# A lambda table made in parts between Vector products, one k copy moved to Scalar and one mask product postponed, in a linear-attention and gated-FFN kernel

## The chip, the cores and the metric

One core of one Trainium2 chip. The metric is the device time of one execution in microseconds (us). The profile names the engines PE (TensorE), DVE (Vector), ACT (Scalar), POOL (GpSimd) and SP. "Span" is the time from the first to the last instruction that the trace shows.

## The reference, cut to what matters

Block-wise linear attention with a decay lambda per head (4 batches, 8 heads, 768 positions, width 64), then a gated feed-forward layer on the result.

```python
Dmask = np.where(rel >= 0, lam[:, None, None] ** rel[None, :, :], 0.0)
lam_pow = lam[:, None, None] ** (pos[None, :, None] + 1)
for b in range(nb):
    intra = np.einsum('bhic,bhjc->bhij', qb, kb) * Dmask[None]
    intra = np.einsum('bhij,bhjd->bhid', intra, vb)
    inter = np.einsum('bhid,bhde->bhie', qb * lam_pow[None], kv_state)
    out[:, :, sl] = intra + inter
    # ... kv_state is decayed and updated
gate = 1.0 / (1.0 + np.exp(-(x @ w_gate)))
val = x @ w_val
return (gate * val @ w_out)
```

## The kernel before

It works on six blocks of 128 positions. q is scaled by a table of powers of lambda, `lamq`. Block 0 has a table of its own; the table for later blocks is made on Vector while the first block's units ("unit tile" = 128 columns of the hidden layer: matmuls g and v, sigmoid, product) run.

```python
def make_lamq():
    lp = const.tile([128, HP, C], FP32, tag="lp")
    for u in range(2):                       # two column copies
        us = slice(u * 64, (u + 1) * 64)
        nc.vector.tensor_copy(lp[us]...[:, :, :, 0], lam_bc[us, :]...[:, u])
    w = 1
    while w < C:                             # seven doublings
        nc.vector.tensor_tensor(out=lp[:, :, w:2 * w], in0=lp[:, :, 0:w],
                                in1=lp[:, :, w - 1:w].to_broadcast([128, HP, w]), op=ALU.mult)
        w *= 2
    nc.vector.tensor_copy(lamq, lp)          # the cast to bf16
# ... the order of block 0
piece_tq0([1]); piece_tk0(0)     # transposes; piece_tk0 copies k to SBUF: i=0 of pair 0 on Vector, else Scalar
make_mask(1); idle(1)
piece_s(0, [0]); piece_m(0, 0)   # scores of batch 0, times the mask (two Vector products)
piece_s(0, [1]); piece_m(0, 1)
piece_tk0(1)
piece_tq0([2]); piece_tq0([3])   # transposes of q and their scaling on Vector
piece_s(0, [2], ps_ff, "ff"); piece_m(0, 2)
piece_s(0, [3]); piece_m(0, 3)
# ... later: GpSimd issues the loads of weights and of block 1, each when an earlier one has landed
load_gv(3, GW); load_gv(4, GW); load(1, "qk", 0, 2); load_gv(5, GW)  # ...
# ... units of block 0
make_lamq()
for ft in (2, 3): gs[ft] = psum(); mm_part(gs[ft], WG, ...); sigm(0, ft, gs[ft])
for ft in (2, 3): vp = psum(); mm_part(vp, WV, ...); prod(0, ft, vp)
g4 = psum(); mm_part(g4, WG, ...); sigm(0, 4, g4)
v4 = psum(); mm_part(v4, WV, ...); prod(0, 4, v4)
```

`psum()` takes a buffer from a pool of three. v4 can start only when the product of tile 2 has been made.

Of the kernel before, what the change touches and what calls it, by code (L numbers as in the profile page):

```python
# [7 lines left out]
FP32 = mybir.dt.float32  # L8
BF16 = mybir.dt.bfloat16
# [6 lines left out]
def kernel(  # L16
# [11 lines left out]
    nc = tc.nc  # L28

    B, H, S, D = q.shape  # L30
    C = 128
    NSTEP = S // C
    HP = H // 2
# [7 lines left out]
    const = ctx.enter_context(tc.tile_pool(name="const", bufs=1))  # L41
# [3 lines left out]
    mtp = ctx.enter_context(tc.tile_pool(name="mtp", bufs=4))  # L45
# [57 lines left out]
    def load_wo(i, w):  # L103
        fs = slice(i * w, (i + 1) * w)
        nc.gpsimd.dma_start(out=WO[:, fs, :], in_=wo_r[:, fs, :])
# [14 lines left out]
    w = 1  # L120
# [38 lines left out]
    for u in range(2):  # L159
        us = slice(u * 64, (u + 1) * 64)  # L160
# [10 lines left out]
    for u in range(2):  # L171
        us = slice(u * 64, (u + 1) * 64)
# [3 lines left out]
    lamq = const.tile([128, HP, C], BF16, tag="lamq")  # L176
    mask = const.tile([128, H, C], FP32, tag="mask")

    def make_lamq():
        lp = const.tile([128, HP, C], FP32, tag="lp")  # L180
        for u in range(2):
            us = slice(u * 64, (u + 1) * 64)
            nc.vector.tensor_copy(lp[us].rearrange("p (e x) c -> p e x c", e=2)[:, :, :, 0],
                                  lam_bc[us, :].rearrange("p (x u e) -> p u e x", u=2, e=2)[:, u])
        w = 1
        while w < C:
            nc.vector.tensor_tensor(out=lp[:, :, w:2 * w], in0=lp[:, :, 0:w],  # L187
                                    in1=lp[:, :, w - 1:w].to_broadcast([128, HP, w]), op=ALU.mult)
            w *= 2
        nc.vector.tensor_copy(lamq, lp)  # L190

    def make_mask(u):
# [4 lines left out]
    def masked(out, x, n, u):  # L197
        if n == 0:
            nc.vector.tensor_tensor(out=out, in0=x, in1=mask[:, u::2, :], op=ALU.mult)  # L199
            return  # L200
        nc.vector.tensor_tensor(  # L201
            out=out.rearrange("p (e x) c -> p e x c", e=2), in0=x.rearrange("p (e x) c -> p e x c", e=2),
            in1=mask.rearrange("p (x u e) c -> p u e x c", u=2, e=2)[:, u], op=ALU.mult)
# [7 lines left out]
    QS, KS, MT, XT, KD = {}, {}, {}, {}, {}  # L211
# [22 lines left out]
    def transpose_pair(out, x, b, g):  # L234
        nc.tensor.transpose(out, x[:, b, 2 * g:2 * g + 2, :].rearrange("p h d -> p (h d)"), ident)
# [7 lines left out]
    def piece_tq0(bs, then=None):  # L243
        tq = ps_at.tile([128, 2, 2, 2 * C], BF16, name="tq", tag="ps")
        for b in bs:
            if (0, b // 2) not in QS:
                QS[0, b // 2] = trsb.tile([128, 2, 2, 2, C], BF16, tag="QS", name="QS")
            for g in range(HP):
                transpose_pair(tq[:, b % 2, g // 2, g % 2 * C:g % 2 * C + C], Q[0], b, g)
        if then:  # L250
            then()
        for b in bs:
            nc.vector.tensor_tensor(out=QS[0, b // 2][:, :, b % 2].rearrange("p e x c -> p e (x c)"),
                                    in0=tq[:, b % 2], in1=lamq0_e, op=ALU.mult)

    def piece_tk0(bp):
        tk = ps_at.tile([128, 2, 2, 2 * C], BF16, name="tk", tag="ps")
        for i in range(2):
            for g in range(HP):
                transpose_pair(tk[:, i, g // 2, g % 2 * C:g % 2 * C + C], K[0], 2 * bp + i, g)  # L260
        KS[0, bp] = trsb.tile([128, 2, 2, 2, C], BF16, tag="KS", name="KS")
        for i in range(2):
            cp = nc.vector.tensor_copy if bp == 0 and i == 0 else nc.scalar.copy
            cp(KS[0, bp][:, :, i].rearrange("p e x c -> p e (x c)"), tk[:, i])

    def piece_t(n, bp):
        if n > 1 or bp == 1:
# [21 lines left out]
    def piece_s(n, bs, pool=ps_at, tag="ps"):  # L289

        for b in bs:
            bp, i = b // 2, b % 2
            sp = [pool.tile([128, HP, C], FP32, name=f"sp{u}", tag=tag) for u in range(2)]
            for hp in range(HP):
                for u in range(2):
                    us = slice(u * 64, (u + 1) * 64)
                    nc.tensor.matmul(sp[u][:, hp, :], lhsT=KS[n, bp][us, hp // 2, i, hp % 2, :],  # L297
                                     rhs=QS[n, bp][us, hp // 2, i, hp % 2, :],
                                     start=(hp == 0), stop=(hp == HP - 1), skip_group_check=True)
            SP[n, b] = sp  # L300

    def piece_m(n, b):
        MT[n, b] = mtp.tile([128, 2, HP, C], BF16, tag="MT", name="MT")
        for u in range(2):
            masked(MT[n, b][:, u], SP[n, b][u], n, u)

    def intra(n, b, out, m, start, stop):
# [68 lines left out]
    def fade():  # L376
        for bp in range(NB2):
            SD[bp] = kdp.tile([128, 2, HP, D], FP32, tag="sd", name="sd", bufs=2)
            nc.gpsimd.tensor_tensor(out=SD[bp], in0=Sb[:, 2 * bp:2 * bp + 2],  # L379
                                    in1=dec.unsqueeze(1).unsqueeze(3).to_broadcast([128, 2, HP, D]),  # L380
                                    op=ALU.mult)
# [6 lines left out]
    def c(n, *pairs):  # L388
        for bp in pairs:
            pool, tag = (ps_at, "ps") if bp == 0 or n == 0 else (ps_ff, "ff")  # L390
            cp = pool.tile([128, 2, HP, D], FP32, name="cp", tag=tag)
            for i in range(2):
                for hp in range(HP):
                    for u in range(2):
                        h = head(hp, u)
                        nc.tensor.matmul(cp[half(u), i, hp, :], lhsT=kdh(n, 2 * bp + i, h),  # L396
                                         rhs=V[n][:, 2 * bp + i, h, :], start=(i == 0 and hp == 0),
                                         stop=(i == 1 and hp == HP - 1), skip_group_check=True)
            dst = Sb[:, 2 * bp:2 * bp + 2]
            if n == 0:  # L400
                nc.vector.tensor_copy(dst, cp)
            else:
                nc.vector.tensor_tensor(out=dst, in0=cp, in1=SD.pop(bp), op=ALU.add)  # L403
# [3 lines left out]
    def piece_gv(n, ft):  # L407
        fs = slice(ft * 128, (ft + 1) * 128)
        x = XT[n].rearrange("p m b c -> p m (b c)")
        gp = ps_ff.tile([128, TCH], FP32, name="gp", tag="ff")  # L410
        for mt in range(NMT):
            nc.tensor.matmul(gp, lhsT=WG[:, mt, fs], rhs=x[:, mt, :],  # L412
                             start=(mt == 0), stop=(mt == NMT - 1))
        sg = htp.tile([128, TCH], BF16, tag="sg", name="sg", bufs=3)
        nc.scalar.activation(sg, gp, AF.Sigmoid)  # L415
        vp = ps_ff.tile([128, TCH], FP32, name="vp", tag="ff")
        for mt in range(NMT):
            nc.tensor.matmul(vp, lhsT=WV[:, mt, fs], rhs=x[:, mt, :],  # L418
                             start=(mt == 0), stop=(mt == NMT - 1))
        HT[n, ft] = htp.tile([128, TCH], BF16, tag="ht", name="ht", bufs=2 * NFT)  # L420
        nc.vector.tensor_mul(HT[n, ft], sg, vp)  # L421

    def mm_part(ps, W, n, ft, lo, hi):
        x = XT[n].rearrange("p m b c -> p m (b c)")
        for mt in range(NMT):
            nc.tensor.matmul(ps[:, lo:hi], lhsT=W[:, mt, ft * 128:(ft + 1) * 128], rhs=x[:, mt, lo:hi],  # L426
                             start=(mt == 0), stop=(mt == NMT - 1))

    def psum():
        return ps_ff.tile([128, TCH], FP32, name="gp", tag="ff")  # L430
# [5 lines left out]
    def prod(n, ft, vp):  # L436
        sg = HT[n, ft]
        HT[n, ft] = htp.tile([128, TCH], BF16, tag="ht", name="ht", bufs=2 * NFT)
        nc.vector.tensor_mul(HT[n, ft], sg, vp)  # L439
# [53 lines left out]
    idle(1)  # L493
    piece_tq0([1])
    piece_tk0(0)
    make_mask(1)
    idle(1)
    piece_s(0, [0])
    piece_m(0, 0)
    piece_s(0, [1])  # L500
    piece_m(0, 1)
    piece_tk0(1)
    nc.scalar.preload_act_table_set("sigmoid_and_others")
    piece_tq0([2])
    piece_tq0([3])
    piece_s(0, [2], ps_ff, "ff")
    piece_m(0, 2)
    piece_s(0, [3])
    piece_m(0, 3)
# [37 lines left out]
    def gv(n, *fts):  # L547
        for ft in fts:
            piece_gv(n, ft)
# [10 lines left out]
    mm_part(v1, WV, 0, 1, 0, TCH)  # L560
    prod(0, 1, v1)
    c(0, 1)
    make_lamq()
    gs = {}
    for ft in (2, 3):
        gs[ft] = psum()
# [2 lines left out]
    for ft in (2, 3):  # L569
        vp = psum()  # L570
        mm_part(vp, WV, 0, ft, 0, TCH)
        prod(0, ft, vp)
    g4 = psum()
    mm_part(g4, WG, 0, 4, 0, TCH)
    sigm(0, 4, g4)
    v4 = psum()
    mm_part(v4, WV, 0, 4, 0, TCH)
    prod(0, 4, v4)
    fade()
    make_kd(1)  # L580
    for i in range(3):
        load_wo(i, NFT // 3)
    gv(0, 5, 6, 7)
    gv(0, 8)
    t(1, 0)
    gv(0, 9)
# [104 lines left out]
```

## Time and profile before

Median 226.81 us of three runs (226.63 to 226.98).

| reading | value | where it is read |
|---|---|---|
| PE busy | 216.0 us of a span of 225.3 (96%) | the page, part 1 |
| PE's share of the chain that ended last | 91% | the page, part 4 |
| largest wait of PE behind 14.7 us | 0.61 us idle, at v of unit tile 4 | the timeline |

From the page of the kernel before, part 1 (busy time, share of the span, instructions) and part 4 (the chain by engine):

```profile
PE 216.0 (96%) x1726; PEld 114.3 (51%) x1748; DVE 106.8 (47%) x193; ACT 79.2 (35%) x149; POOL 78.5 (35%) x77
PE 91%; DVE 3%; DMA 3%; issue 2%; ACT 1%; DVEq 0%; POOLq 0%
```

The timeline of the same run around the table. Columns: start, duration (us), engine, source line, operation, output<-inputs, count, and in brackets the idle time before it and what ended it.

```profile
19.13 0.88 POOL L85 DMA_DIRECT2D qb<-in_q_dram  x1 [0.64 <-DMA WG<-in_moe_w_gate_dram]
20.23 0.87 POOL L85 DMA_DIRECT2D qb<-in_q_dram  x1 [0.23 <-DMA WV<-in_moe_w_val_dram]
20.58 0.68 DVE L183 COPY lp<-lam_bc 64x4 f32<-64x4 f32 x2
21.29 1.84 DVE L187 TENSOR_TENSOR lp<-lp 128x4 f32<-128x4 f32 x7
22.93 0.87 POOL L85 DMA_DIRECT2D kb<-in_k_dram  x1 [0.48 <-DMA WV<-in_moe_w_val_dram]
23.17 0.85 DVE L190 CAST lamq<-lp 128x512 bf16<-128x512 f32 x1
23.95 1.26 DVE L439 TENSOR_TENSOR ht<-sg,gp 128x512 bf16<-128x512 bf16 x2
24.67 1.02 PE L426 MATMUL gp<-XT,WV 128*128 128x512 bf16 x4 [0.61 <-DVE ht L439]
```

Read from the bottom: v4 waited for the product of tile 2, which waited behind the cast. A later section returns to the POOL lines and to the first column copy, which taken alone lasted 0.50 us while its twin of the same shape took 0.17:

```profile
20.58 0.50 DVE L183 COPY lp<-lam_bc 64x4 f32<-64x4 f32 x1
```

The timeline of block 0 in the same run (`tk` transposed k in PSUM, `KS` its copy, `sp` scores, `MT` masked scores, `QS` scaled q), up to the first unit matmul:

```profile
7.39 0.62 PE L235 MATMUL tk<-ident,kb 128*128 128x128 bf16 x8 [0.27 <-DMA kb<-in_k_dram]
8.04 0.42 DVE L264 COPY KS<-tk 128x512 bf16<-128x512 bf16 x1 [0.38 <-PE tk L235]
8.50 0.59 ACT L264 COPY KS<-tk 128x512 bf16<-128x512 bf16 x1 [1.33 <-DVE KS L264]
8.98 2.48 DVE L199 TENSOR_TENSOR MT<-sp,mask 128x512 bf16<-128x512 f32 x4
11.38 0.75 DVE L253 TENSOR_TENSOR QS<-tq,lamq 128x512 bf16<-128x512 bf16 x2
11.85 0.73 PE L297 MATMUL sp<-QS,KS 64*128 64x128 bf16 x16 [0.69 <-DVE QS L253]
12.26 2.48 DVE L199 TENSOR_TENSOR MT<-sp,mask 128x512 bf16<-128x512 f32 x4
14.70 0.49 PE L426 MATMUL gp<-XT,WG 128*128 128x384 bf16 x2
```

Vector is almost never free here; between 11.38 + 0.75 and 12.26 it waited 0.13 us for scores.

### The profile page before, as it was taken

To read this page: it belongs to the slowest core of one execution; us is meant where nothing else is said; L and a number is where in the kernel's file an instruction comes from. 1 tells how busy PE (TensorE), PEld (TensorE's weight loads), DVE (VectorE), ACT (ScalarE), POOL (GpSimd) and SP (SyncE) were. 2 spreads that over 40 slices of the span, in tenths; PEclk is the share of its full clock that TensorE was granted. 3 is DMA by queue.
4 is the path that set the end of the run, shared out by engine and by line. 5 is a ranking of instruction groups with operands and counts; after the bars stand their busy time and mean duration, and the time that the engine had idled before them with its cause. 6 is when DMAs were issued, how large, how long until landed. Compare 5 with 4: busy or idle time off the path is not lost.

```text
span 225.3 us, 4243 instructions
## 1 busy us (share of the span) xinstructions
PE 216.0 (96%) x1726; PEld 114.3 (51%) x1748; DVE 106.8 (47%) x193; ACT 79.2 (35%) x149; POOL 78.5 (35%) x77
## 2 busy tenths in 40 slices
PE   6689899999999999999999999999999999999994
PEld 2454355888854455444545444446444445444443
DVE  7898646586430622435732345742334850333300
ACT  5554234444422225333215333225333224333221
POOL 8996687973691007940005950000000000000000
PEclk9999999999999999999999999999999999999999
DMA  6999999999999992999021999021940012100022
GB/s 111 155 173 195 189 175 155 151 197 169 157 185 186 209 174 86 206 154 118 1 96 47 234 136 144 1 96 47 129 108 0 0 49 93 47 3 0 0 93 95
DMA packets 105891, 25.70 MB, mean 114 GB/s; under 512 B 96016, under 2 KB 102928, under 8 KB 105872
## 3 DMA queue, kind: packets, MB, share of 16 engines
q0 software_dynamic: 81264, 13.90, 79.7%
q1 hardware_dynamic: 23568, 11.28, 20.5%
q10 hardware_dynamic: 1040, 0.26, 0.5%
q8 instruction: 13, 0.21, 0.4%
q14 instruction: 6, 0.05, 0.1%
HBM read 28.32 MB, written 6.29 MB: 154 GB/s over the span
## 4 chain that ended last, share of the span: by engine, by line
PE 91%; DVE 3%; DMA 3%; issue 2%; ACT 1%; DVEq 0%; POOLq 0%
PE po L475 27%; PE gp L412 21%; PE vp L418 20%; PE gp L447 5%; PE vp L453 5%; PE sp L297 3%; PE gp L426 3%; PE op L309 3%; DMA kb<-in_k_dram 3%; PE op L321 1%; PE po L464 1%; PE cp L396 1%; DVE MT L199 1%; DVE lp L187 1%; DVE ht L439 1%
## 5 line engine op out<-in xcount | busy, mean ns | idle before, releaser
L421 DVE TENSOR_TENSOR ht<-sg,vp 128x512 bf16<-128x512 bf16 x54 | 37.2, 688 | 65.2 <-PE vp L418 60.0
L475 PE MATMUL po<-WO,ht 128*128 128x512 bf16 x266 | 61.3, 379 | 0.5
L412 PE MATMUL gp<-XT,WG 128*128 128x512 bf16 x211 | 55.0, 379 | 0.6 <-issue 0.2
L418 PE MATMUL vp<-XT,WV 128*128 128x512 bf16 x211 | 54.3, 379 | 0.0
L415 ACT ACTIVATE sg<-gp 128x512 bf16<-128x512 f32 x54 | 32.2, 597 | 59.8 <-PE gp L412 59.8
L475 PEld LDWEIGHTS <-ht 128*128 128x128 bf16 x276 | 26.3, 98 | 31.0
L418 PEld LDWEIGHTS <-WV 128*128 128x128 bf16 x216 | 21.1, 98 | 25.5
L412 PEld LDWEIGHTS <-WG 128*128 128x128 bf16 x216 | 20.8, 98 | 24.7
L478 ACT COPY ob<-po 128x512 f32<-128x512 f32 x23 | 13.5, 586 | 52.2 <-PE po L475 48.4
L201 DVE TENSOR_TENSOR MT<-sp,mask 128x512 bf16<-128x512 f32 x40 | 25.2, 683 | 10.2 <-PE sp L297 10.2
L379 POOL TENSOR_TENSOR sd<-Sb,dec 128x512 f32<-128x512 bf16 x8 | 8.2, 1044 | 43.4 <-DVE Sb L403 43.3
L447 PE MATMUL gp<-XT,WG 128*128 128x256 bf16 x96 | 14.4, 273 | 0.0
L453 PE MATMUL vp<-XT,WV 128*128 128x256 bf16 x96 | 14.4, 273 | 0.0
L457 DVE TENSOR_TENSOR ht<-sg,vp 128x256 bf16<-128x256 bf16 x24 | 10.0, 420 | 8.6 <-PE vp L453 8.6
L450 ACT ACTIVATE sg<-gp 128x256 bf16<-128x256 f32 x24 | 9.2, 384 | 13.0 <-PE gp L447 11.8
L91 POOL DMA_DIRECT2D vb<-in_v_dram x10 | 12.8, 1281 | 0.8 <-DMA WG<-in_moe_w_gate_dram 0.6
L370 POOL TENSOR_TENSOR kd<-kb,kds 128x1024 bf16<-128x1024 bf16 x6 | 11.3, 1905 | 3.4 <-PE gp L447 3.4
L403 DVE TENSOR_TENSOR Sb<-cp,sd 128x512 bf16<-128x512 f32 x8 | 5.2, 686 | 15.5 <-PE cp L396 15.5
L336 ACT CAST XT<-op 128x512 bf16<-128x512 f32 x19 | 9.9, 598 | 2.1 <-PE op L309 2.0
L447 PEld LDWEIGHTS <-WG 128*128 128x128 bf16 x96 | 9.2, 98 | 1.7 <-issue 0.2
L453 PEld LDWEIGHTS <-WV 128*128 128x128 bf16 x96 | 9.4, 98 | 1.1
L77 POOL DMA_DIRECT2D qb<-in_q_dram x8 | 9.4, 1185 | 0.0
(80 smaller groups left out, 160.4 us busy)
## 6 DMA issues: line engine op xcount, KB each, us to landing
out_dram<-ob SPq DMA_DIRECT2D x21, 256.0 KB, 2.0
kb<-in_k_dram POOLq DMA_DIRECT2D x10, 256.0 KB, 8.4
qb<-in_q_dram POOLq DMA_DIRECT2D x8, 256.0 KB, 8.3
vb<-in_v_dram POOLq DMA_DIRECT2D x4, 512.0 KB, 13.1
WO<-in_moe_w_out_dram POOLq DMA_DIRECT2D x3, 512.0 KB, 8.7
WG<-in_moe_w_gate_dram POOLq DMA_DIRECT2D x5, 256.0 KB, 8.5
WV<-in_moe_w_val_dram POOLq DMA_DIRECT2D x5, 256.0 KB, 9.4
qb<-in_q_dram POOLq DMA_DIRECT2D x6, 128.0 KB, 8.4
```

Source lines behind the costliest of these rows:

```text
L91: nc.gpsimd.dma_start(out=lst[n][:, b0:b1], in_=src[b0:b1, :, sl, :].rearrange("b h s d -> s (b h) d"))
L201: nc.vector.tensor_tensor(out=out.rearrange("p (e x) c -> p e x c", e=2), in0=x.rearrange("p (e x) c -> p e x c", e=2), in1=mask.rearrange ...
L370: nc.gpsimd.tensor_tensor(out=KD[n][:, e], in0=K[n][:, e], in1=kds[:, e::2].unsqueeze(1).unsqueeze(3).to_broadcast([128, B, HP, D]), op=AL ...
L412: nc.tensor.matmul(gp, lhsT=WG[:, mt, fs], rhs=x[:, mt, :], start=(mt == 0), stop=(mt == NMT - 1))
L415: nc.scalar.activation(sg, gp, AF.Sigmoid)
L418: nc.tensor.matmul(vp, lhsT=WV[:, mt, fs], rhs=x[:, mt, :], start=(mt == 0), stop=(mt == NMT - 1))
L421: nc.vector.tensor_mul(HT[n, ft], sg, vp)
L447: nc.tensor.matmul(gp[:, cs], lhsT=WG[:, mt, fs], rhs=x[:, mt, cs], start=(mt == 0), stop=(mt == NMT - 1))
L453: nc.tensor.matmul(vp[:, cs], lhsT=WV[:, mt, fs], rhs=x[:, mt, cs], start=(mt == 0), stop=(mt == NMT - 1))
L457: nc.vector.tensor_mul(HT[n, ft][:, cs], sg[:, cs], vp[:, cs])
L475: nc.tensor.matmul(po, lhsT=HT[n, ft][:, tt * 128:(tt + 1) * 128], rhs=WO[:, ft, :], start=(ft == 0), stop=(ft == NFT - 1))
L478: nc.scalar.copy(ob, po)
```

## The change

The intent: Vector's products of the units no longer queue behind the whole table; and in block 0 Vector is relieved of a copy, and the last q's are scaled earlier so that the last scores come earlier.

```diff
-    def make_lamq():
-        lp = const.tile([128, HP, C], FP32, tag="lp")
+    lp = const.tile([128, HP, C], FP32, tag="lp")
+    def lamq_start():        # the two column copies
+    def lamq_double(*ws):    # doublings ws
+    def lamq_end():          # the cast
     ... (bodies as before)
-            cp = nc.vector.tensor_copy if bp == 0 and i == 0 else nc.scalar.copy
-            cp(KS[0, bp][:, :, i]..., tk[:, i])
+            nc.scalar.copy(KS[0, bp][:, :, i]..., tk[:, i])
     ...
-    piece_m(0, 1)
+    piece_m(0, 1, (0,))
     piece_tk0(1)
     piece_tq0([2])
     piece_tq0([3])
+    piece_m(0, 1, (1,))
     ...
-    make_lamq()
+    lamq_start()
     ... (g and v of tiles 2 and 3, products 2 and 3)
+    lamq_double(1, 2, 4, 8)
     ... (g, v and product of tile 4)
+    lamq_double(16, 32, 64)
     ...
-    gv(0, 5, 6, 7)
+    gv(0, 5)
+    lamq_end()
+    gv(0, 6, 7)
```

More of the change, by code (lines that the diff above doesn't have):

```diff
@@ L184, in make_lamq @@
                                   lam_bc[us, :].rearrange("p (x u e) -> p u e x", u=2, e=2)[:, u])
-        w = 1
-        while w < C:
+    def lamq_double(*ws):
+        for w in ws:
             nc.vector.tensor_tensor(out=lp[:, :, w:2 * w], in0=lp[:, :, 0:w],
                                     in1=lp[:, :, w - 1:w].to_broadcast([128, HP, w]), op=ALU.mult)
-            w *= 2
+    def lamq_end():
         nc.vector.tensor_copy(lamq, lp)
@@ L262, in piece_tk0 @@
         for i in range(2):
-            cp = nc.vector.tensor_copy if bp == 0 and i == 0 else nc.scalar.copy
-            cp(KS[0, bp][:, :, i].rearrange("p e x c -> p e (x c)"), tk[:, i])
+            nc.scalar.copy(KS[0, bp][:, :, i].rearrange("p e x c -> p e (x c)"), tk[:, i])
     def piece_t(n, bp):
@@ L300, in piece_s, with piece_m @@
             SP[n, b] = sp
-    def piece_m(n, b):
-        MT[n, b] = mtp.tile([128, 2, HP, C], BF16, tag="MT", name="MT")
-        for u in range(2):
+    def piece_m(n, b, us=(0, 1)):
+        if us[0] == 0:
+            MT[n, b] = mtp.tile([128, 2, HP, C], BF16, tag="MT", name="MT")
+        for u in us:
             masked(MT[n, b][:, u], SP[n, b][u], n, u)
```

## The prediction

> **What bounds the kernel now.** TensorE. The page has PE busy 216.0 of a 225.3 us span (96%) and 91% of the chain of waits. In the timeline of PE alone, matmuls of 512 columns start every 0.216 us from 14.70 us to the end. Only one later stall has a releaser other than "issue" and is over 0.1 us: at 24.67 us (v of unit tile 4) PE was idle 0.61 us, released by "DVE ht L439"; against the 0.216 us rhythm it started 0.77 us late. Before 14.70 us lies a chain of short steps between DMA, PE, DVE and ACT.
>
> **Part 1, the lambda table.** v4 needs the PSUM buffer that the product of tile 2 frees (three buffers in that ring). v2 was finished at 22.33, but DVE, in order, was in the table from 20.58 to 24.03: two column copies (0.68 in all), seven doublings (0.17 to 0.43 each, 1.84 together, each idle about 34 ns for the one before), a cast of 0.86; the product ran 23.95 to 24.62. The Trainium skill (VectorE: DVE Perf Modes, "The DRAIN you can't avoid") says that a read of what the previous Vector instruction wrote needs a semaphore; the trace agrees, every doubling waits for its forerunner. Nothing is removed, only moved. With the new order I place product 2 at about 22.4 to 23.1 (right behind v2), product 3 behind v3, doublings 1 to 8 (0.8) and 16 to 64 (1.05) and the cast (0.86) each in the gap of about 1.0 us between products. PE's buffer is free at 23.1, v4 would start at 23.90. The table is first read at 33.3 (scaling of block 1) and is done at about 28.3: no new wait. Gain: 0.77 us, all on the chain, because PE streams from there on and the loads behind it (weights, block 1) land at least 0.3 us before use even when PE is 0.8 earlier.
>
> **Part 2, block 0.** Vector loses one copy (0.42) and the Scalar copy no longer waits for it (ACT waited 1.33, released by "DVE KS L264"). But the first copy is on Scalar 0.59, so the first half of the k tile is ready at 8.64 in place of 8.47, and the first score matmuls start about 8.69 in place of 8.52; the second half stays at 9.1. The mask product then starts at about 9.13 (was 8.98): the Vector time that was saved falls in a wait for PE. The scaled q of batch 2 and 3 come about 0.45 earlier, which closes Vector's 0.14 gap at 12.26. But the postponed mask product frees, at about 12.28, the PSUM buffer of the second half of the last scores; those start at 12.34 in place of 12.18, and PE is in order. So the last steps (op, XT copy, first unit matmul at 14.70) come about 0.16 us LATER. Loads don't hide it: the first gate weights land at 14.0.
>
> **Sum.** -0.77 + 0.16 = about -0.6 us of 226.81: 226.2 us. Range 225.7 to 226.7. Faster by over 2%: 0.01; within 2%: 0.98; slower by over 2%: 0.01.
>
> **What would show it.** Right: no PE gap at v4, L439 products evenly spaced, span shorter by about 0.6; first matmul of the unit at about 14.86. Wrong in part 1: a new PE wait on "DVE ht" among tiles 4 to 6, or a later DMA wait that eats the gain. Wrong in part 2: the first unit matmul at or before 14.70.
>
> **What would make it wrong.** Vector may have been closer to the limit in block 0 than I think (then part 2 gains 0.1 to 0.2 too: 225.9); small drifts of DMA landings, which are not fixed from run to run, are of the size of the effect; a doubling that straddles a product delays it by up to 0.1.

## The result, and the profile after

Median 226.55 us (226.47 to 227.21, six runs) against 226.95 us for the kernel before in the same rounds (226.63 to 226.99, six runs). The ratio is 0.999, with a 95% interval of 0.9977 to 1.0002: no difference that these rounds resolve. A ratio here is the mean time of one kernel's fast runs over that of the other's in the same rounds, so it is not quite the ratio of the medians. By means the difference is 0.24 us, by medians 0.40; the forecast was 0.61.

Yet the two traces differ by 0.8 us of span, 225.3 against 224.5. So the first question is not only "why less than 0.6", but also "why does the trace show more than the clock".

The page of the changed kernel, parts 1 and 4:

```profile
PE 218.5 (97%) x1748; PEld 114.6 (51%) x1748; DVE 105.5 (47%) x192; ACT 79.6 (35%) x150; POOL 78.4 (35%) x77
PE 94%; DMA 3%; DVE 1%; issue 1%; ACT 1%; POOLq 0%
```

(1748 instead of 1726 matmuls is not more work: 22 matmul records are missing from the first trace.) Its timeline around the table:

```profile
20.55 0.34 DVE L184 COPY lp<-lam_bc 64x4 f32<-64x4 f32 x2
22.41 0.69 DVE L442 TENSOR_TENSOR ht<-sg,gp 128x512 bf16<-128x512 bf16 x1 [1.53 <-PE gp L429]
23.28 0.69 DVE L442 TENSOR_TENSOR ht<-sg,gp 128x512 bf16<-128x512 bf16 x1 [0.18 <-PE gp L429]
23.87 1.03 PE L429 MATMUL gp<-XT,WV 128*128 128x512 bf16 x4
23.88 0.80 DVE L189 TENSOR_TENSOR lp<-lp 128x4 f32<-128x4 f32 x4
25.00 0.69 DVE L442 TENSOR_TENSOR ht<-sg,gp 128x512 bf16<-128x512 bf16 x1 [0.32 <-PE gp L429]
25.61 0.54 DVE L189 TENSOR_TENSOR lp<-lp 128x64 f32<-128x64 f32 x2
```

The product of tile 2 comes at 22.41 and v4 at 23.87 with no idle time before it, as predicted to within 0.03 us. And its block 0:

```profile
7.49 0.62 PE L238 MATMUL tk<-ident,kb 128*128 128x128 bf16 x8 [0.44 <-DMA kb<-in_k_dram]
8.15 1.07 ACT L266 COPY KS<-tk 128x512 bf16<-128x512 bf16 x2 [1.04 <-PE tk L238]
9.22 1.89 DVE L202 TENSOR_TENSOR MT<-sp,mask 128x512 bf16<-128x512 f32 x3 [0.75 <-PE sp L299]
11.03 0.75 DVE L256 TENSOR_TENSOR QS<-tq,lamq 128x512 bf16<-128x512 bf16 x2
11.49 0.73 PE L299 MATMUL sp<-QS,KS 64*128 64x128 bf16 x16 [0.24 <-DVE QS L256]
11.69 3.07 DVE L202 TENSOR_TENSOR MT<-sp,mask 128x512 bf16<-128x512 f32 x5
14.68 0.49 PE L429 MATMUL gp<-XT,WG 128*128 128x384 bf16 x2
```

Here the prediction is plainly wrong. The first k happened to land 0.10 us later in this run, and still the first unit matmul is not later: measured from the first k transpose it comes after 7.19 us, before after 7.31. The last scores (the second eight of the sixteen at L299) did not stop for the postponed mask product.

### The profile page after: what moved, and what is told of

It reads as the page before. It is cut to its first block, busy times and chain, and to the rows that moved or that the text cites. A ratio compares the mean times of both kernels' runs of the same rounds, so it can differ in the third digit from the quotient of the medians.

```text
span 224.5 us, 4265 instructions
## 1 busy us (share of the span) xinstructions
PE 218.5 (97%) x1748; PEld 114.6 (51%) x1748; DVE 105.5 (47%) x192; ACT 79.6 (35%) x150; POOL 78.4 (35%) x77
## 4 chain that ended last, share of the span: by engine, by line
PE 94%; DMA 3%; DVE 1%; issue 1%; ACT 1%; POOLq 0%
PE po L478 27%; PE gp L415 21%; PE vp L421 21%; PE gp L450 5%; PE gp L429 5%; PE vp L456 5%; PE op L312 3%; PE sp L299 3%; DMA kb<-in_k_dram 3%; PE op L324 1%; PE cp L399 1%; PE po L467 1%; DVE MT L202 1%; PE tk L238 0%; ACT XT L352 0%
## 5 line engine op out<-in xcount | busy, mean ns | idle before, releaser
L478 PE MATMUL po<-WO,ht 128*128 128x512 bf16 x276 | 62.0, 380 | 0.0
L421 PE MATMUL vp<-XT,WV 128*128 128x512 bf16 x216 | 55.4, 379 | 0.0
```

The source lines that it names most:

```text
L421: nc.tensor.matmul(vp, lhsT=WV[:, mt, fs], rhs=x[:, mt, :], start=(mt == 0), stop=(mt == NMT - 1))
L478: nc.tensor.matmul(po, lhsT=HT[n, ft][:, tt * 128:(tt + 1) * 128], rhs=WO[:, ft, :], start=(ft == 0), stop=(ft == NFT - 1))
```

## The experiments

Two intervals of PE separate the parts of the change from the luck of a run. **Interval A** runs from the first k transpose to the first unit matmul (block 0's part). **Interval B** runs from the first unit matmul to the first q transpose of block 1 (it holds the units of block 0, so the table's stall). Both are differences of starts that the timeline prints to 0.01 us, so the last digit can be off by one. From that transpose to the last matmul PE took 189.79 or 189.80 us in every trace but one (e6, told there), so all else is in A, B and the landing of the first k.

### The parts taken one by one

e1 is the changed kernel again. e2 has only the table in parts:

```diff
 (against the changed kernel)
+            cp = nc.vector.tensor_copy if bp == 0 and i == 0 else nc.scalar.copy
+            cp(KS[0, bp][:, :, i]..., tk[:, i])
-            nc.scalar.copy(KS[0, bp][:, :, i]..., tk[:, i])
-    piece_m(0, 1, (0,))
+    piece_m(0, 1)
-    piece_m(0, 1, (1,))
```

e3 has only block 0's part, the table in one piece:

```diff
 (against the changed kernel)
     lamq_start()
+    lamq_double(1, 2, 4, 8, 16, 32, 64)
+    lamq_end()
     ... (the three later calls removed)
```

e4 is the changed kernel with the first k copy left on Vector:

```diff
 (against the changed kernel)
+            cp = nc.vector.tensor_copy if bp == 0 and i == 0 else nc.scalar.copy
+            cp(KS[0, bp][:, :, i]..., tk[:, i])
-            nc.scalar.copy(KS[0, bp][:, :, i]..., tk[:, i])
```

> The changed kernel again, in more rounds. Theory A (the two profiles tell the truth: 225.3 against 224.5 us of span, the stall of 0.77 us at v of unit tile 4 gone, block 0 even): the mean of the fast runs is 0.6 to 0.9 us under that of the kernel before, ratio 0.996 to 0.9975. Rival B (the profiled run of the kernel before was itself slow, 227.44 against a timed median of 226.95, so that the profiles overstate): 0.2 to 0.5 us, ratio 0.998 to 0.999.

> The table in parts, block 0 as before. Theory A: v of tile 4 follows g of tile 4 with no idle, all of the gain is here: 0.7 to 0.8 us under before, the first unit matmul stays at 14.6 to 14.8 us. My prediction on record would have it 0.16 us better than the whole change.

> Block 0 changed, the table in one piece as before. Prediction on record: 0.16 us slower than before, first unit matmul at 14.86. Theory A (the second half of the last scores does not use the buffer of the postponed mask product but that of the k transposes, so nothing waits): the first unit matmul comes 0 to 0.15 us earlier relative to the landing of the first k, the whole within 0.15 us of before, and the stall of about 0.6 us idle at v of tile 4 remains.

> The whole change, but with the first k copy left on Vector. If the copy on Scalar delays the first mask product by 0.15 us, as I predicted and as the trace of the change seems to show (first scores 1.30 us behind the first k transpose, before 1.13), the first mask product starts 0.15 us earlier behind the transpose than in the changed kernel, and the first unit matmul up to 0.1 us earlier; the time is then at or up to 0.15 us under the changed kernel. Rival: the load of the third v (lands at 13.3) bounds and nothing moves.

Measured, ratio to the kernel before (median 227.01 us of 11 runs), and the intervals of the trace:

| run | median us | ratio, 95% interval | A us | B us |
|---|---|---|---|---|
| kernel before, first trace | – | – | 7.31 | 17.74 |
| changed kernel, first trace | – | – | 7.19 | 16.96 |
| e1 changed kernel | 226.94 | 0.9993 (0.9975 to 1.0011) | 7.19 | 16.96 |
| e2 table only | 226.63 | 0.9984 (0.9968 to 1.0001) | 7.31 | 16.97 |
| e3 block 0 only | 226.84 | 0.9997 (0.9977 to 1.0016) | 7.18 | 17.26 |
| e4 copy left on Vector | 226.78 | 0.9988 (0.9970 to 1.0006) | 7.16 | 17.05 |

The times tell nothing apart; the intervals do. First, block 0's part is a gain of about 0.13 us, not a loss of 0.16. Second, e3 has the table in one piece, as before, but its B is only 0.30 above that of the changed kernel, not 0.77. So the stall that I had costed was not a constant of the kernel. e3's timeline shows what differs:

```profile
20.45 0.34 DVE L184 COPY lp<-lam_bc 64x4 f32<-64x4 f32 x2
20.82 1.85 DVE L189 TENSOR_TENSOR lp<-lp 128x4 f32<-128x4 f32 x7
22.33 0.88 POOL L85 DMA_DIRECT2D kb<-in_k_dram  x1 [0.47 <-DMA WG<-in_moe_w_gate_dram]
22.71 0.72 DVE L193 CAST lamq<-lp 128x512 bf16<-128x512 f32 x1
```

The doublings take the same 1.85 us. But the copies took 0.34 where the first trace had 0.68, and the cast 0.72 where it had 0.85, and 0.42 in the changed kernel. Each long one began while GpSimd was in the middle of issuing a load. (e4's B is 0.09 us above 16.96 without a stall at v4: its units start so early that PE met two loads of weights that had just landed, at 15.59 and 19.43 us.) Two expectations were missed in the times: e1's ratio lies above the ranges of both of its theories, and e2 gained 0.44 us in the mean where theory A had 0.7 to 0.8.

### Theory and rival

The Trainium skill (SBUF — State Buffer, "Who interferes with whom") says that Vector and GpSimd share a pair of SBUF ports, that whichever takes it first holds it for its whole instruction while the other fully blocks, that Vector's `copy` and `cast` can enter a mode that needs it, and that `tensor_tensor` has no such mode (with both inputs in SBUF it contends only with what GpSimd reads there). The same page ("SBUF: two separate sides") says that the descriptors of a load issued by GpSimd are written by GpSimd, through that pair.

- **Lock theory:** the stall is nothing but the time that the table's copies and cast stood waiting for a GpSimd issue. It changes with the phase of the issues.
- **Rival (the prediction's view):** Vector's own work in the table makes the stall; its length is fixed.

e5 is the kernel before again. e6 keeps the table in one piece but lets GpSimd go on with its issues only when the table is finished:

```diff
-    load(1, "qk", 0, 2)          # and load_gv(5), load(1, "v", ...), load(1, "qk", 2, 4), moved down
     ...
     make_lamq()
+    jp = const.tile([128, 1], BF16, tag="jp")
+    nc.gpsimd.tensor_copy(jp, lamq[:, 0, 0:1])
+    load(1, "qk", 0, 2)          # and the others
```

e7 and e8 put the same small copy and the loads behind the fifth (w = 16) or the sixth (w = 32) doubling, reading `lp`, so that an issue meets the cast.

> The kernel before against itself: the floor of the comparison (ratio 1.000 within its interval of about 0.0015), and a second trace of it. Lock theory: a Vector copy or cast of the table that starts while GpSimd is busy issuing a load ends only with that issue (so far 0.03 us before its end for the column copy, 0.23 us after it for the cast), else takes 0.15 and 0.42 us; the stall of PE at v of unit tile 4 equals the excess over 0.15 and 0.42 (0.79 of excess against 0.77 of stall in the first trace, 0.30 against 0.30 in e3_block0_only). It depends on the phase of the issues in that run, anything from 0 to 0.8 us. Rival (my prediction): Vector's work in the table itself makes the stall, then it is near 0.77 us again in every run.

> The kernel before with its table in one piece, but GpSimd's issues of the loads of block 1 wait until the table is finished (a one-column copy of the table on GpSimd stands ahead of them). Lock theory: column copies 0.15 us, cast 0.42 us, and the stall of PE at v of unit tile 4 is under 0.1 us although the table was not split. Rival (the length of the table's own work): the stall stays at 0.3 to 0.8 us. Beware: the loads come later, so a new wait may appear at the transposes of block 1 (from 32 us); that would be a separate thing.

> The same, but GpSimd is let go by the fifth doubling, so that its first issue of about 0.87 us runs on into the cast. Lock theory: the cast ends 0.23 us after the issue does, so it takes 0.42 to 0.6 us, stall at v of tile 4 of 0 to 0.15 us. Rival: cast and stall as in e6.

> The same, let go by the sixth doubling: the issue starts some 0.2 us ahead of the cast. Lock theory: cast 0.8 to 1.0 us, stall at v of tile 4 about 0.4 to 0.55 us, with the same Vector instructions as e6. If the issue starts behind the cast, the cast takes 0.42 us and the issue is what waits. Rival: cast and stall as in e6.

The timeline of e6:

```profile
21.34 0.34 DVE L183 COPY lp<-lam_bc 64x4 f32<-64x4 f32 x2
21.70 1.84 DVE L187 TENSOR_TENSOR lp<-lp 128x4 f32<-128x4 f32 x7
23.58 0.43 DVE L190 CAST lamq<-lp 128x512 bf16<-128x512 f32 x1
24.32 1.77 POOL L85 DMA_DIRECT2D qb<-in_q_dram  x2
24.66 1.02 PE L426 MATMUL gp<-XT,WV 128*128 128x512 bf16 x4
```

The table was not split, Vector does the same instructions, and v4 starts with no idle time: B is 16.97. The rival, that the length of the table's work alone makes the stall, falls here. The DMA engines moved 195 GB/s while this table was made (21.3 to 24.0 us) and 196 GB/s around the table of the first trace (20.5 to 24.1), so it is GpSimd's issuing that counts, and not the traffic of loads. That the shared ports are the reason is the skill's account; the runs show only who held up whom. In e7, with the two issues that begin at 23.06, one met the cast:

```profile
23.06 1.77 POOL L85 DMA_DIRECT2D qb<-in_q_dram  x2
23.57 0.60 DVE L198 CAST lamq<-lp 128x512 bf16<-128x512 f32 x1
24.81 1.02 PE L434 MATMUL gp<-XT,WV 128*128 128x512 bf16 x4
```

The cast took 0.60, 0.17 more, and B is 17.14, 0.17 more. e8 failed as a dose: the issue began at 23.50, only 0.05 us ahead of the cast, and the cast won (0.43 us, B 16.97). It was then the issue that grew: it took 0.96 us, the next one 0.89. The expectation had allowed for this only for an issue that starts behind the cast.

As a comparison of times e6 is spoiled: it is 0.23% slower than before (ratio 1.0023, 1.0003 to 1.0043). In e6, e7 and e8 the first k landed at 8.0 us, in the other traces at 7.29 to 7.66, with GpSimd issuing it at the same 1.26 us; their A was 7.39 to 7.41 us, with block 0 unchanged. The edit lies far behind that point. Why it lands late in all three I can't say; e6 also took 0.19 us more behind block 1's first transpose, which I did not follow up.

e5, the kernel before against itself, gave 0.9988 (0.9971 to 1.0005). That is the floor: the same code seems 0.27 us faster than itself, about as much as the changed kernel did.

### Taking the lock out without splitting, and a better version

e9 leaves block 0 as before and the doublings in one piece, but has the column copies on Scalar, early, and the cast on Scalar behind the sigmoid of tile 4. e10 adds the postponed mask product of the change, with the first k copy left on Vector.

```diff
+        nc.scalar.copy(lp[us]...[:, :, :, 0], lam_bc[us, :]...[:, u])    # in the set-up
-        nc.vector.tensor_copy(lp[us]...[:, :, :, 0], lam_bc[us, :]...[:, u])
-        nc.vector.tensor_copy(lamq, lp)
     sigm(0, 4, g4)
+    nc.scalar.copy(lamq, lp)
     (e10 also:)
-    piece_m(0, 1)
+    piece_m(0, 1, (0,))
     piece_tq0([3])
+    piece_m(0, 1, (1,))
```

> The kernel before, block 0 untouched, GpSimd's issues untouched, the seven doublings in one piece where they stood; only the two column copies go to Scalar (in its idle time at 7.2 us) and the cast to Scalar behind the sigmoid of tile 4. Lock theory: Scalar and the two-input doublings don't wait for GpSimd, so the stall of PE at v of unit tile 4 is gone whatever the phase of the issues: 16.95 to 17.0 us from the first unit matmul to the first transpose of block 1, as with the table in three parts. My prediction's view, that the table must be broken up, would leave some 0.2 us or more. Time: as e2_table_only, 0.2 to 0.5 us under before in the mean.

> e9 with the postponed mask product of block 0 (first k copy left on Vector): meant to beat both kernels. Stall gone, first unit matmul 7.20 us behind the landing of the first k (7.36 before, 7.23 in the changed kernel, 7.20 in e4). Time 0.3 to 0.6 us under before in the mean, 0 to 0.2 under the changed kernel, which the rounds can hardly resolve.

> The changed kernel once more, on the same chip as e9 and e10. Stall gone in the profile again; mean 0.2 to 0.5 us under before. Some single runs of either kernel will be 0.6 us longer with the first k landing that much later (as in e6 to e8), which is not the change.

> A third trace of the kernel before. Lock theory: stall at v of tile 4 equals the excess of the table's copies and cast over 0.15, 0.17 and 0.42 us, within 0.05 us, whatever it is this time (0.77 and 0.31 so far).

The timeline of e9, with an issue in progress during most of the doublings:

```profile
20.83 1.84 DVE L188 TENSOR_TENSOR lp<-lp 128x4 f32<-128x4 f32 x7
20.84 0.87 POOL L85 DMA_DIRECT2D qb<-in_q_dram  x1 [0.44 <-DMA WV<-in_moe_w_val_dram]
22.18 0.87 POOL L85 DMA_DIRECT2D kb<-in_k_dram  x1 [0.47 <-DMA WG<-in_moe_w_gate_dram]
24.14 1.03 PE L426 MATMUL gp<-XT,WV 128*128 128x512 bf16 x4
24.97 0.62 ACT L576 CAST lamq<-lp 128x512 bf16<-128x512 f32 x1
```

B is 16.96, no stall, with no doubling moved, and the doublings take their 1.84 us whatever GpSimd does. (e9 also gives Vector less to do, so alone it would not exclude the rival; e6 does.) The most telling trace is that of e12, the unchanged kernel before:

```profile
20.57 0.33 DVE L183 COPY lp<-lam_bc 64x4 f32<-64x4 f32 x2
20.70 0.87 POOL L85 DMA_DIRECT2D qb<-in_q_dram  x1 [0.35 <-DMA WV<-in_moe_w_val_dram]
20.94 1.85 DVE L187 TENSOR_TENSOR lp<-lp 128x4 f32<-128x4 f32 x7
22.04 0.88 POOL L85 DMA_DIRECT2D kb<-in_k_dram  x1 [0.47 <-DMA WG<-in_moe_w_gate_dram]
22.82 0.43 DVE L190 CAST lamq<-lp 128x512 bf16<-128x512 f32 x1
23.16 1.28 DVE L439 TENSOR_TENSOR ht<-sg,gp 128x512 bf16<-128x512 bf16 x2
23.90 1.02 PE L426 MATMUL gp<-XT,WV 128*128 128x512 bf16 x4
```

By luck the first copy fell between two issues, the second began just 0.04 us behind an issue and won, and the cast began 0.10 us before the issue of 22.04 was recorded as over, yet lost nothing. The kernel before has no stall at all here, and its span is 224.5 us, the same as that of the changed kernel.

Times: e9 median 226.32 (ratio 0.9970, 0.9952 to 0.9988), e10 226.40 (0.9970, 0.9952 to 0.9987), e11 226.73 (0.9986, 0.9968 to 1.0004), the kernel before 226.97. The leads of e9 and e10, 0.65 and 0.68 us in the mean, are above what was expected of them. Intervals: e10 has A 7.15 and B 17.00 (its B met a load of weights, as e4's did), e11 A 7.18 and B 16.97. So the postponed mask product alone gives A of 7.15 or 7.16 (e10, e4); the moved k copy gives back 0.03 of that. Because the control was as far from 1 as the change, a last round repeated e10, the changed kernel and the kernel before.

> e10 once more. If its lead is its own, the mean of the fast runs is again 0.5 to 0.8 us under before and 0.2 to 0.5 under the changed kernel. If it was chance of the loads, it comes to within 0.2 us of the changed kernel. In the trace: no stall at v of tile 4 (16.95 to 17.0 us from first unit matmul to the first transpose of block 1), first unit matmul 7.20 us behind the landing of the first k.

> The changed kernel beside it: 0.2 to 0.4 us under before in the mean; in the trace no stall, first unit matmul 7.23 us behind the landing of the first k.

> The kernel before against itself again: if the 0.9988 of e5 was noise, the ratio is now on either side of 1 within 0.0015; whatever it is, it is the size of difference that these rounds can't tell. In the trace the stall at v of tile 4 again equals the excess of the table's copies and cast over 0.15, 0.17 and 0.42 us within 0.05 us.

| run | median us | ratio, 95% interval | A us | B us |
|---|---|---|---|---|
| e13 version of e10 | 226.21 | 0.9977 (0.9962 to 0.9993) | 7.12 | 17.43 |
| e14 changed kernel | 227.03 | 1.0023 (0.9995 to 1.0051) | 7.18 | 16.96 |
| e15 kernel before | 226.93 | 1.0011 (0.9992 to 1.0031) | 7.32 | 17.05 |

In e14 two of six runs were at a granted clock of 0.984 and 0.985 (228.21 and 228.39 us), which spoils its mean. In e13's trace B holds 0.39 us of idle time at the v of tile 1, released by a weight load; it landed late, at 18.48 us, in that run, and it has nothing to do with the table.

The version of e10 was under the kernel before in both rounds, with intervals that exclude 1. e9, which leaves block 0 alone, had the same ratio in its one round, so these rounds do not tell the two apart. But the lead of e10 is not what I designed. In every run of e9, e10 and e13 the time is 1.73 to 1.85 us longer than the span; in all the other timed runs about 2.1 (2.05 to 2.21). So some 0.3 us of the lead lie outside the span that the trace shows, and no view tells why. Inside the span, e10 leads the changed kernel of the same round (e11) by 0.05 us, 224.62 against 224.67 in the mean of six runs.

### The stall, trace by trace

"Excess" is what the two copies and the cast took over 0.33 and 0.43 us, the values of e12. "Stall" is B less 16.96, the value with no idle time.

| trace, table in one piece on Vector | copies + cast us | excess us | stall us |
|---|---|---|---|
| before, first trace | 0.68 + 0.85 | 0.77 | 0.78 |
| e5 before again | 0.65 + 0.43 | 0.32 | 0.32 |
| e12 before, one look | 0.33 + 0.43 | 0 | 0 |
| e15 before again | 0.34 + 0.51 | 0.09 | 0.09 |
| e3 block 0 only | 0.34 + 0.72 | 0.30 | 0.30 |
| e6 issues held | 0.34 + 0.43 | 0.01 | 0.01 |
| e7 issue into the cast | 0.34 + 0.60 | 0.18 | 0.18 |
| e8 issue into the cast, lost | 0.33 + 0.43 | 0 | 0.01 |

The stall is the excess, to 0.01 us, over a range of 0 to 0.78. Why one for one? Because the table's own work, which cost PE nothing by itself, had used up all the slack. Behind the first unit matmul the product of tile 2 starts after 7.73 us in the changed kernel, and after 8.46 in e12, where it waits for a table without excess; it ends at 23.84 there, and v4 starts at 23.90, on time. In the first trace v4 starts as closely behind that product (24.62 and 24.67). So any excess goes straight to PE. The split does not keep the issues away from the copies and the cast; it gives the slack back. e1 shows it: its copies took 0.61 us (0.28 of excess) and its cast 0.87 (0.44), yet its B is 16.96:

```profile
27.55 0.87 DVE L193 CAST lamq<-lp 128x512 bf16<-128x512 f32 x1
```

In the four traces of the kernel before the stall averages 0.30 us (0.78, 0.32, 0 and 0.09).

## Why the prediction was right or wrong

- **"What bounds the kernel now. TensorE"**: right. Behind 14.7 us PE streams, and A, B and the first landing account for the span.
- **"Gain: 0.77 us, all on the chain"**: the place was right (v4, waiting for the product of tile 2, waiting for the table), and the gain does reach the end: B fell to 16.96. The mis-sized term is the 0.77. I took one trace's stall for a constant. It measured 0.78, 0.32, 0 and 0.09 us in four traces of the same kernel, 0.30 in the mean, because it is the time for which copies and cast waited for GpSimd's issues. The clue was in my own numbers: "two column copies (0.68 in all)" was one of 0.50 and one of 0.17 with the same shape, and no idle time was listed before the first. I also entered the cast at 0.86 us in the new order; it took 0.42 in the first trace of the changed kernel, where no issue met it, and 0.87 in e1, where one did, without harm to PE in either.
- **"the postponed mask product frees [...] the PSUM buffer of the second half of the last scores"**: wrong, and with it the "+0.16". I had assumed that the pool of five hands out its buffers in a fixed rotation. The compiled programs of both kernels (as building them again shows) place the last scores in banks 0 and 1: bank 0 was held by the first half of batch 1's scores, bank 1 by the second k transposes, which Scalar's copies free. The postponed mask product frees bank 4, which the first `op` tile had before; in the changed kernel that tile has bank 3. So the pool reuses what the program frees first. The last scores follow at once on the q's, and the mask product fills Vector's gap. Instead of 0.16 us later, the first unit matmul came about 0.13 us earlier behind the first k transpose (A 7.19 in e1, 7.18 in e3 and e14; 7.31 and 7.32 before).
- **"the first half of the k tile is ready at 8.64"**: right in kind. Against e4, where the first k copy stays on Vector, the changed kernel's A is 0.03 us longer, though the first mask product comes 1.73 us behind the first k transpose instead of 1.60. Vector catches up later. In e4 (and e10) the chain of waits to the first unit matmul runs back to the second load of v, landing at 12.44 us (12.41), and no longer to k; that limits what the earlier start is worth.
- **"226.2 us. Range 225.7 to 226.7"**: the range held 226.55, but that was partly luck: the forecast difference of 0.6 us was not met (0.24 by means, 0.40 by medians), and its two errors have opposite signs (0.77 for a stall of 0.30 in the mean, +0.16 for a gain of 0.13). Worked out from the traces, an average run should gain about 0.30 + 0.13 = 0.43 us; that is an estimate from four traces. The timed rounds gave ratios of 0.9990, 0.9993, 0.9986 and 1.0023 for the changed kernel and 0.9988 and 1.0011 for the kernel before against itself. So the estimate is not confirmed by the clock: what the change is worth in a mean run stays open between 0 and about 0.5 us. Traces show that its two mechanisms work.
- **"small drifts of DMA landings [...] are of the size of the effect"**: right, and larger than I thought: the first k landed anywhere from 7.29 to 8.01 us.

Why did the first pair of traces show 0.8 us? The first trace of the kernel before was the worst of four (stall 0.78); its profiled run was indeed 227.44 us, against a timed median of 226.81.

## What to carry to other kernels

When two Vector instructions of one shape differ in duration, look at what GpSimd was doing: in these traces the time that a copy or cast stood blocked appears as a longer instruction and not as a wait, and what stands behind it is then blamed on Vector. Before costing a stall from one trace, see whether its length is fixed or depends on the phase of something (take a second trace); if it is a lottery, the gain is its mean, and moving the few copies and casts to Scalar can do as much as rearranging the work. And don't guess which PSUM buffer a tile gets: read it from the compiled program, or from whom the matmul waits for.

## What the Trainium skill lacked or had wrong

- SBUF — State Buffer ("Who interferes with whom"): it says who blocks whom, and for the whole instruction, but not where in an instruction's recorded window the lock lies; by the recorded windows, which are rough for GpSimd, the lock is shorter than the issue. Here Vector won when it began 0.04 (e12), 0.05 (e8), 0.07 and 0.20 (e5) or 0.12 us (e14) behind the recorded start of an issue, and lost from 0.24 us on (first trace). Blocked casts ended 0.22 to 0.23 us behind the recorded end of the issue (first trace, e1, e3, e7, e15) and blocked column copies 0.03 us before it (first trace, e1, e5, e14), as if the ports came free about 0.19 us before that end (an estimate: 0.42 less 0.23 for the cast, 0.15 plus 0.03 for the copy).
- The same page gives only as inferred why `tensor_tensor` and descriptor writing leave each other alone. The runs agree that they do: the seven doublings took 1.84 or 1.85 us in each trace with the table's doublings in one piece, with or without an issue in progress.
- Perfetto Trace Analysis: I found no hint there that such a lock shows as the loser's duration (cast 0.42 to 0.87 us for the same shape) while the view of waits names only the Vector product behind it ("DVE ht L439").
- No page that I read tells of the landing of the first load drifting by up to 0.7 us with the same issue time (7.3 us in most traces, 8.0 in e6 to e8), nor of a time outside the span that differs by 0.3 us between builds (1.8 us in e9, e10 and e13; 2.1 in the others). Both stay unexplained here.
